# K of a group in one load of 64 KB rows: three neighbouring pages, and a branch on TensorE that picks the second

## The chip, the cores and the metric

The kernel runs on one core of a Trainium2 chip, as one launch. The metric is the device time of that launch in microseconds (us).

## The reference

One decode step (one token, D = 512) of a gated mix of two blocks: attention over a long cache, and a SwiGLU feed-forward block.

```python
g = sigmoid((x * gate_w).sum(-1, keepdims=True))
q = (x @ wq)                      # 32 heads of 128; 8 groups, 4 heads share one K and V
scores = einsum(q, k) * 128**-0.5 # k_cache: 8 groups x 32768 positions x 128, bf16
o = einsum(softmax(scores), v)    # v_cache: the same shape
a = o @ wo                        # wo: 4096 x 512
b = (silu(x @ w_gate) * (x @ w_up)) @ w_down
out = g * a + (1 - g) * b         # 1 x 1 x 512, bf16
```

K and V of one group are 8 MB each (32768 x 128 in bf16), so 128 MB of the 148 MB that the kernel reads are the two caches.

## The kernel before, in words

**Tiling.** A group's K is seen as 128 partitions of 256 positions each, in two halves b = 0, 1 of R = 128 positions per partition. One half of one tensor is a *page*: 32 KB in each partition, 4 MB. The tile `page` holds five pages. K has pages 0 and 1 (`PG_K`), one for each half; V has pages 2 and 3 (`PG_V`); w_gate and w_up start in page 3 (`PG_F`), and page 4 (`PG_X`) holds wq first and wo at the end.

**Loads.** All come from SyncE's queue (SP), in an order written by hand: wq, x, gate_w, w_gate, w_up; then for each group g K half 0, K half 1 (`load_k(g, b)`, L263), V (`load_v(g)`, L274, one load of both pages; the last group's V is two loads, L280); then w_down (L295) and wo in five parts (L301). SP waits before a load until its page is free: `load_k(g, b)` waits for the fill that ends half b of group g-1 (`sem_fill`), and `load_v(g)` waits until TensorE has ended the V matmuls of group g-1 (`sem_v_free`). A wait on SP holds every load behind it.

**A group on the engines.** TensorE (`emit_k`, once for each half) takes a half in UPP = 8 units. A unit is a *fill* (`emit_fill`, L309: 8 transposes of 128 x 128 FP32 words, each a pair of bf16 values, into one of two PSUM tiles `pst`) and, LAG = 2 units later, its *scores* (`emit_scores`, L321: 16 small matmuls into the PSUM bank `ps_sc[b]`). Between them VectorE copies the PSUM tile into `ktT` (L635). Each half ends with two units of scores alone, since its last two copies have to come back first. VectorE then takes the half's maximum (L640). After both halves come the maximum over partitions (`emit_max`: L343, L347 on TensorE with L650, L654 on VectorE between), the bias `nbias` on ScalarE (L516), eight exponentials of 128 x 128 on ScalarE (L523, four for each half), 64 V matmuls of 128 x 512 (`emit_v`, L362), and a small reduction (`emit_reduce`: L374, L383). TensorE works strictly in this order, so a group's fills begin after the reduction of the group before.

**Loops.** TensorE, VectorE and ScalarE each run the eight groups as a loop in registers, `Fori(0, G*STEP, STEP)` with STEP = 16; semaphores count on, and a wait compares with the loop's register plus a constant. TensorE's code for the end (`emit_end`: w_down, L214, and the first part of wo) stands ahead of that for the start in the program, and is reached in a second turn of an outer loop.

**The end.** w_down's matmuls, the scaled heads (L668, L678, L685, L687), the matmuls with wo in five parts (L214, L225), one ScalarE copy (L697), one VectorE copy (L699) and the output's load to DRAM (L701).

Of the kernel before, what the change touches and what calls it, by code (L numbers as in the profile page):

```python
# [5 lines left out]
ACT = mybir.ActivationFunctionType  # L6
ALU = mybir.AluOpType
# [5 lines left out]
def bass_gated_mix__gqa_block_cached__swiglu_ffn__decode_kernel(  # L13
# [26 lines left out]
    R = 128  # L40
# [27 lines left out]

    PG_K = (0, 1)
    PG_V = 2  # L70
    PG_F = 3
    PG_X = 4
    NPG = 5

    with ExitStack() as es:
# [57 lines left out]
        def T(name, shape, dt):  # L133
            return es.enter_context(nc.sbuf_tensor(name, shape, dt))
# [26 lines left out]
        nbias = T("nbias", [128, HPG], FP32)  # L161
        esum = T("esum", [128, NB, HPG], FP32)
        esum2 = T("esum2", [128, HPG], FP32)
        acc = T("acc", [128, RQ, DH], FP32)
# [10 lines left out]

        ps_sc = [P(f"ps_sc{i}", [128, 512], FP32) for i in range(NB)]
        ps_o = P("ps_o", [128, 512], FP32)
# [27 lines left out]

        vpage = page[:, PG_V : PG_V + NB, :].rearrange("p b (r d) -> p b r d", d=DH)
        wq_v = page[:, PG_X, 0 : KC * H * DH].rearrange("p (c n) -> p c n", c=KC)
        wgu = page[:, PG_F, 0 : 2 * KC * F].rearrange("p (w c f) -> p w c f", w=2, c=KC)
# [39 lines left out]
        with nc.Block("main") as block:  # L248
            @block.gpsimd
            def _(pool):  # L250
                pool.memset(ones_f[:, :], 1.0).then_inc(sem_ones, 1)
                pool.memset(ones_bf[:, :], 1.0).then_inc(sem_ones, 1)
                for g in range(G - 1):
                    pool.wait_ge(sem_v[0], 16 * (g + 1))
                    pool.sem_inc(sem_v[1], 16)

            @block.sync
            def _(sp):
                def load_k(g, b):
                    if g:  # L260
                        sp.wait_ge(sem_fill, UPG * (g - 1) + UPP * (b + 1))
                    src = A_k_cache[0, g, :, :].rearrange("(p b r) d -> p b r d", b=NB, r=R)
                    sp.dma_start(  # L263
                        page[:, PG_K[b], :].rearrange("p (r d) -> p r d", d=DH), src[:, b, :, :]
                    ).then_inc(sem_k[b], 16)

# [24 lines left out]
                for g in range(G):  # L291
                    for b in range(NB):
                        load_k(g, b)
                    load_v(g)
                sp.dma_start(  # L295
                    wd[:, :, :], B_w_down.rearrange("(p j) n -> p j n", j=FC)
# [7 lines left out]
            def _(pe):  # L304
                def emit_fill(b, u):
                    kv = page[:, PG_K[b], :].bitcast(FP32)
                    for k in range(RPU):
                        n = u * RPU + k
                        ins = pe.transpose(  # L309
                            pst[u % NST][:, k * 128 : (k + 1) * 128],  # L310
                            kv[:, n * 128 : (n + 1) * 128],
                            ident_f[:, :],
                        )
                    ins.then_inc(sem_fill, 1)
# [14 lines left out]

                def emit_k(i, b):  # L330
                    pe.wait_ge(sem_k[b], i + 16)
                    for u in range(UPP + LAG):
                        if u >= LAG:
                            pe.wait_ge(sem_cp, i + (UPP * b + u - LAG + 1))
                        if u < UPP:
                            emit_fill(b, u)
                        if u >= LAG:
                            ins = emit_scores(b, u - LAG)
                    ins.then_inc(sem_sc, UPP)

# [51 lines left out]
                def emit_start():  # L392
# [86 lines left out]
                    with pe.Fori(0, G * STEP, STEP) as i:  # L479
                        for b in range(NB):  # L480
                            emit_k(i, b)
                        emit_max(i)
                        emit_v(i)
                        emit_reduce(i)
# [21 lines left out]
            def _(act):  # L506
# [5 lines left out]
                act.activation(sg, pst[1][:, 0:FS], ACT.Sigmoid).then_inc(sem_act_sg, 1)  # L512

                with act.Fori(0, G * STEP, STEP) as i:
                    act.wait_ge(sem_b, i + STEP)
                    act.activation(  # L516
                        nbias[:, :], ps_m[:, M_B0 : M_B0 + HPG], ACT.Copy, scale=-SCALE
                    ).then_inc(sem_nbias, STEP)
                    act.wait_ge(sem_nbias, i + STEP)
                    for b in range(NB):  # L520
                        sc = ps_sc[b][:, :].rearrange("p (t h) -> p h t", h=HPG)
                        for h in range(HPG):
                            act.activation(  # L523
                                ET[:, b * R : (b + 1) * R, h],
                                sc[:, h, :],
                                ACT.Exp,
# [8 lines left out]
            def _(dve):  # L535
# [95 lines left out]
                with dve.Fori(0, G * STEP, STEP) as i:  # L631
                    for b in range(NB):
# [101 lines left out]
```

## Time and profile before

| what | value |
|---|---|
| median of 3 runs | 351.63 us (351.47 to 351.8) |
| the profiled execution's own time | 351.67 us |
| its span in the profile | 350.4 us (the other 1.27 us lie around it) |
| DMA queue of SP | 148.12 MB, 98.4% of 16 engines' span; 423 GB/s mean |
| TensorE matmul / weight load busy | 73% / 60% |
| VectorE, ScalarE busy | 55%, 12% |
| mean granted TensorE clock | 0.864 of full speed |

The table's shares are means over the whole span. What ends last differs from stage to stage, and within a group TensorE's, VectorE's and ScalarE's work is a chain: a share of 73% does not say how long that chain is.

### The profile page before, as it was taken

How to read it: one execution, taken by the hardware profiler on the slowest of the kernel's cores; microseconds unless marked ns; L12 is line 12 of the kernel's file. 1: busy time of each engine (PE TensorE's matmuls, PEld its weight loads, DVE VectorE, ACT ScalarE, POOL GpSimd, SP SyncE). 2: the span in 40 equal slices, each digit the busy share in tenths (PEclk: the TensorE clock that was granted, in tenths of full speed). 3: DMA queues.
4: the chain of work that ended last, by engine and by line, in shares of the span. 5: the costliest groups of instructions: out<-in, count | busy, mean ns of one | idle time of the engine just before them, and what ended most of it. 6: DMA issues, size and time to landing. Idle time of an engine off the chain costs nothing.

```text
span 350.4 us, 8660 instructions
## 1 busy us (share of the span) xinstructions
PE 254.6 (73%) x3871; PEld 209.2 (60%) x3871; DVE 192.1 (55%) x242; ACT 42.9 (12%) x156; POOL 0.4 (0%) x6
## 2 busy tenths in 40 slices
PE   1443986688857994898858993798768893798574
PEld 1113985288725984398726991498627891498431
DVE  4243986068803885068804892088705891198500
ACT  1000000400050002300050005000050005000130
POOL 0000000000000000000000000000000000000000
PEclk9965999699968997689969997889859995899878
DMA  8999999999989999999999999999999999999995
GB/s 337 408 451 419 477 443 384 423 430 456 464 385 417 456 426 430 423 464 434 434 404 419 464 449 400 423 449 434 434 419 419 464 434 415 423 426 434 420 423 205
DMA packets 4914, 148.21 MB, mean 423 GB/s; under 512 B 554, under 2 KB 556, under 8 KB 940
## 3 DMA queue, kind: packets, MB, share of 16 engines
q1 hardware_dynamic: 4908, 148.12, 98.4%
q8 instruction: 5, 0.08, 0.1%
q14 instruction: 1, 0.01, 0.0%
HBM read 148.11 MB, written 0.00 MB: 423 GB/s over the span
## 4 chain that ended last, share of the span: by engine, by line
DMA 69%; PE 25%; DVE 3%; SPq 1%; ACT 1%; issue 1%; DVEq 0%; ACTq 0%
DMA page<-in_A_k_cache_dram 56%; PE pst L309 18%; DMA page<-in_A_wo_dram 12%; PE ps_sc L321 5%; DVE ktT L635 2%; PE ps_o L362 2%; SPq L301 0%; ACT ET L523 0%; ACT L516 0%; SPq L288 0%; SPq L280 0%; DVE pmaxf L640 0%; PE ps_m L347 0%; SPq L295 0%; PE ps_sc L225 0%
## 5 line engine op out<-in xcount | busy, mean ns | idle before, releaser
L635 DVE COPY ktT<-pst 128x2048 bf16<-128x2048 bf16 x128 | 155.4, 1223 | 31.1 <-PE pst L309 23.4
L309 PE MATMUL pst<-ident_f,page 128*128 128x128 f32 x1024 | 140.5, 286 | 15.6 <-DMA page<-in_A_k_cache_dram 10.3
L309 PEld LDWEIGHTS pst<-ident_f,page 128*128 128x128 f32 x1024 | 115.9, 146 | 19.8 <-DMA page<-in_A_k_cache_dram 11.0
L321 PE MATMUL ps_sc<-qcur,ktT 128*128 128x8 bf16 x2048 | 67.8, 166 | 8.6 <-DVE ktT L635 8.6
L321 PEld LDWEIGHTS ps_sc<-qcur,ktT 128*128 128x128 bf16 x2048 | 66.7, 97 | 11.2 <-DVE ktT L635 10.0
L362 PE MATMUL ps_o<-page,ET 128*16 128x512 bf16 x512 | 43.6, 515 | 27.1 <-ACT ET L523 27.1
L362 PEld LDWEIGHTS ps_o<-page,ET 128*16 128x16 bf16 x512 | 15.8, 113 | 51.5 <-issue 36.4
L516 ACT ACT_TABLE_LOAD x8 | 10.3, 1283 | 239.0 <-PE ps_m L347 239.0
L658 DVE TENSOR_TENSOR esum<-esum 128x4 f32<-128x4 f32 x8 | 1.3, 164 | 42.7 <-ACT ET L523 42.7
L523 ACT ACTIVATE ET<-ps_sc,nbias 128x128 bf16<-128x128 f32 x64 | 23.9, 562 | 0.7
L662 DVE RECIPROCAL rS<-ps_sc 128x4 f32<-128x4 f32 x8 | 1.5, 182 | 34.2 <-PE ps_sc L374 34.2
L523 ACT ACTIVATION_READ_ACCUMULATOR ET<-ps_sc,nbias 128x1 f32 x64 | 18.6, 290 | 0.0
L640 DVE TENSOR_REDUCE pmaxf<-ps_sc 128x4 f32<-128x512 f32 x16 | 11.1, 692 | 10.4 <-PE ps_sc L321 10.4
L383 PE MATMUL ps_m<-sel,acc 128*128 128x4 f32 x64 | 8.4, 255 | 3.6 <-ACT acc L532 3.6
L383 PEld LDWEIGHTS ps_m<-sel,acc 128*128 128x128 f32 x64 | 7.7, 191 | 4.3 <-ACT acc L532 4.3
L343 PE MATMUL ps_m<-ident_f,pmax 128*4 128x128 f32 x8 | 2.5, 308 | 9.1 <-DVE pmax L642 9.1
L532 ACT ACTIVATE acc<-ps_o 128x512 f32<-128x512 f32 x8 | 4.8, 597 | 34.5 <-PE ps_o L362 34.5
L347 PE MATMUL ps_m<-diag,ones_f 4*128 4x4 f32 x16 | 3.6, 294 | 6.3 <-DVE diag L654 6.3
L347 PEld LDWEIGHTS ps_m<-diag,ones_f 4*128 4x128 f32 x16 | 3.2, 244 | 8.1 <-issue 8.1
L404 PE MATMUL ps_m<-ones_bf,x_row 1*128 1x1 bf16 x4 | 0.3, 172 | 9.3 <-DMA x_row<-in_A_x_dram 9.3
L343 PEld LDWEIGHTS ps_m<-ident_f,pmax 128*4 128x4 f32 x8 | 0.6, 81 | 9.6 <-issue 9.6
L404 PEld LDWEIGHTS ps_m<-ones_bf,x_row 1*128 1x128 bf16 x4 | 0.2, 114 | 9.6 <-DMA x_row<-in_A_x_dram 9.6
(68 smaller groups left out, 53.8 us busy)
## 6 DMA issues: line engine op xcount, KB each, us to landing
page<-in_A_k_cache_dram SPq DMA_DIRECT2D x16, 4096.0 KB, 27.4
page<-in_A_v_cache_dram SPq DMA_DIRECT2D x2, 4096.0 KB, 27.3
page<-in_A_wq_dram SPq DMA_DIRECT2D x1, 4096.0 KB, 12.3
page<-in_A_wo_dram SPq DMA_DIRECT2D x1, 2048.0 KB, 40.2
page<-in_B_w_gate_dram SPq DMA_DIRECT2D x1, 1792.0 KB, 15.5
page<-in_B_w_up_dram SPq DMA_DIRECT2D x1, 1792.0 KB, 19.4
wd<-in_B_w_down_dram SPq DMA_DIRECT2D x1, 1792.0 KB, 35.8
page<-in_A_wo_dram SPq DMA_DIRECT2D x1, 1024.0 KB, 42.3
```

The lines of the kernel that those rows point to most:

```text
L309: ins = pe.transpose(pst[u % NST][:, k * 128 : (k + 1) * 128], kv[:, n * 128 : (n + 1) * 128], ident_f[:, :],)
L321: ins = pe.matmul(ps_sc[b][:, col : col + 2 * HPG], kt[:, k, e, :], qcur[:, e, :], start=(e == 0), stop=(e == 1),)
L343: pe.transpose(ps_m[0:HPG, M_A0 : M_A0 + 128], pmax[:, :], ident_f[:, :]).then_inc(sem_t, STEP)
L347: pe.matmul(ps_m[:, M_B0 : M_B0 + HPG], ones_f[0:HPG, :], diag[:, :], start=True, stop=True,).then_inc(sem_b, STEP)
L362: ins = pe.matmul(ps_o[32 * c : 32 * c + RQ * HPG, :], ET[:, n : n + RQ, :].rearrange("p n h -> p (n h)"), vpage[:, b, k * RQ : (k + 1) * ...
L383: ins = pe.matmul(ps_m[:, M_P0 : M_P0 + HPG], acc[:, q, :], sel4[:, q * HPG : (q + 1) * HPG], start=(q == 0), stop=(q == RQ - 1),)
L516: act.activation(nbias[:, :], ps_m[:, M_B0 : M_B0 + HPG], ACT.Copy, scale=-SCALE).then_inc(sem_nbias, STEP)
L523: act.activation(ET[:, b * R : (b + 1) * R, h], sc[:, h, :], ACT.Exp, bias=nbias[:, h : h + 1], scale=SCALE, accum_out=esum[:, b, h : h + ...
L532: act.activation(part, ps_o[:, :], ACT.Copy).then_inc(sem_acc, STEP)
L635: dve.tensor_copy(ktT[:, u % NKT, :], pst[u % NST][:, :].bitcast(BF16)).then_inc(sem_cp, 1)
L640: dve.tensor_reduce(pmaxf[:, b, :], sc, AX.X, ALU.max).then_inc(sem_d, 1)
L662: dve.reciprocal(rS[:, :], ps_s).then_inc(sem_d, 1)
```

## The change

K of a group becomes one load of both halves, with 64 KB rows, for the groups 0 to 6. K now moves among three neighbouring pages A, B, C (0, 1, 2): an even group lies in B and C, an odd group in A and B. Page B is always worked on first. So in an odd group half 1 (page B) comes first and half 0 (page A) second. V and the feed-forward weights move up by a page, wq lies in page A and wo in page C.

- `load_k(g)` waits for the fill that ends the first-worked half of group g-1 (the same value as half 0's wait before). The last group's K is still two loads, half 1 first; the second waits for one more fill.
- GpSimd raises `sem_k[1]` when the whole load has raised `sem_k[0]`, as it did for V.
- SP waits for the fills of the groups 0 to 6 before w_down, because wo now lies in a page of K.
- TensorE runs one pipeline over 18 steps for both halves: the LAG of the first half is no longer drained at the half's end, so that unit 6's and 7's scores come after the fills 8 and 9. The second half's code stands twice in the loop, one copy for page C and one for page A, each behind an `If` on the loop register's parity.
- ScalarE picks the PSUM bank of each exponential by a register (`odd`), since the bank of half 0 changes with parity.
- `nbias` moves from ScalarE (`ACT.Copy`) to VectorE, behind `diag`; a dummy exponential (`eone`) ahead of ScalarE's loop. In the built program the activation-table load that stood in ScalarE's loop, ahead of `nbias`, now stands once ahead of the loop. Each of the eight exponentials gets a register instruction ahead of it.

```diff
-    PG_K = (0, 1)
-    PG_V = 2
-    PG_F = 3
-    PG_X = 4
+    PG_A, PG_B, PG_C = 0, 1, 2
+    PG_V = 3
+    PG_F = 4
+    PG_Q = PG_A
+    PG_X = PG_C
...
-        ps_sc = [P(f"ps_sc{i}", [128, 512], FP32) for i in range(NB)]
+        ps_all = P("ps_sc", [128, NB, 512], FP32)
+        ps_sc = [ps_all[:, b, :] for b in range(NB)]
...
                 for g in range(G - 1):
-                    pool.wait_ge(sem_v[0], 16 * (g + 1))
-                    pool.sem_inc(sem_v[1], 16)
+                    for s in (sem_k, sem_v):
+                        pool.wait_ge(s[0], 16 * (g + 1))
+                        pool.sem_inc(s[1], 16)
...
-                def load_k(g, b):
+                def load_k(g):
                     if g:
-                        sp.wait_ge(sem_fill, UPG * (g - 1) + UPP * (b + 1))
+                        sp.wait_ge(sem_fill, UPG * (g - 1) + UPP)
+                    lo = PG_A if g % 2 else PG_B
+                    dst = page[:, lo : lo + NB, :].rearrange("p b (r d) -> p b r d", d=DH)
                     src = A_k_cache[0, g, :, :].rearrange("(p b r) d -> p b r d", b=NB, r=R)
-                    sp.dma_start(
-                        page[:, PG_K[b], :].rearrange("p (r d) -> p r d", d=DH), src[:, b, :, :]
-                    ).then_inc(sem_k[b], 16)
+                    if g < G - 1:
+                        sp.dma_start(
+                            dst.rearrange("p b r d -> p (b r d)"),
+                            src.rearrange("p b r d -> p (b r d)"),
+                        ).then_inc(sem_k[0], 16)
+                    else:
+                        for n, b in enumerate((1, 0)):
+                            if n:
+                                sp.wait_ge(sem_fill, UPG * (g - 1) + UPP + 1)
+                            sp.dma_start(dst[:, b, :, :], src[:, b, :, :]).then_inc(
+                                sem_k[n], 16
+                            )
...
                 for g in range(G):
-                    for b in range(NB):
-                        load_k(g, b)
+                    load_k(g)
                     load_v(g)
+                sp.wait_ge(sem_fill, UPG * (G - 1))
...
-                def emit_k(i, b):
+                def emit_k(i, b, pg):
                     pe.wait_ge(sem_k[b], i + 16)
-                    for u in range(UPP + LAG):
-                        if u >= LAG:
-                            pe.wait_ge(sem_cp, i + (UPP * b + u - LAG + 1))
-                        if u < UPP:
-                            emit_fill(b, u)
-                        if u >= LAG:
-                            ins = emit_scores(b, u - LAG)
-                    ins.then_inc(sem_sc, UPP)
+                    for n in range(UPP * b, UPP * (b + 1) + LAG * (b == NB - 1)):
+                        if n >= LAG:
+                            pe.wait_ge(sem_cp, i + (n - LAG + 1))
+                        if n < UPG:
+                            emit_fill(pg, n % UPP)
+                        if n >= LAG:
+                            ins = emit_scores((n - LAG) // UPP, (n - LAG) % UPP)
+                            if (n - LAG) % UPP == UPP - 1:
+                                ins.then_inc(sem_sc, UPP)
...
-                        for b in range(NB):
-                            emit_k(i, b)
+                        emit_k(i, 0, PG_B)
+                        with pe.If((i & STEP) < 1):
+                            emit_k(i, 1, PG_C)
+                        with pe.If((i & STEP) > 0):
+                            emit_k(i, 1, PG_A)
...
+                act.wait_ge(sem_ones, 2)
+                act.activation(eone[:, :], ones_f[:, 0:1], ACT.Exp)
...
-                    act.wait_ge(sem_b, i + STEP)
-                    act.activation(
-                        nbias[:, :], ps_m[:, M_B0 : M_B0 + HPG], ACT.Copy, scale=-SCALE
-                    ).then_inc(sem_nbias, STEP)
                     act.wait_ge(sem_nbias, i + STEP)
+                    odd = (i & STEP) * (R // STEP)
+                    sc = ps_all[:, :, :].rearrange("p b (t h) -> p h (b t)", h=HPG)
                     for b in range(NB):
-                        sc = ps_sc[b][:, :].rearrange("p (t h) -> p h t", h=HPG)
+                        bank = R - odd if b else odd
...
-                                sc[:, h, :],
+                                sc[:, h, bass.ds(bank, R)],
...
+                    dve.wait_ge(sem_b, i + STEP)
+                    dve.tensor_scalar(
+                        nbias[:, :], ps_m[:, M_B0 : M_B0 + HPG], -SCALE, None, op0=ALU.mult
+                    ).then_inc(sem_nbias, STEP)
```

More of the change, by code (lines that the diff above doesn't have):

```diff
@@ L67, in bass_gated_mix__gqa_block_cached__swiglu_ffn__decode_kernel @@
     assert QT == 2 and QN == 512 and F % (NSTRIP * FC) == 0 and FS <= 512
-    PG_K = (0, 1)
-    PG_V = 2
-    PG_F = 3
-    PG_X = 4
+    PG_A, PG_B, PG_C = 0, 1, 2
[3 more added lines that the diff above has]
+    PG_X = PG_C
     NPG = 5
+    assert G % 2 == 0
     with ExitStack() as es:
@@ L162, in bass_gated_mix__gqa_block_cached__swiglu_ffn__decode_kernel @@
         esum = T("esum", [128, NB, HPG], FP32)
+        eone = T("eone", [128, 1], FP32)
         esum2 = T("esum2", [128, HPG], FP32)
@@ L206, in bass_gated_mix__gqa_block_cached__swiglu_ffn__decode_kernel @@
         vpage = page[:, PG_V : PG_V + NB, :].rearrange("p b (r d) -> p b r d", d=DH)
-        wq_v = page[:, PG_X, 0 : KC * H * DH].rearrange("p (c n) -> p c n", c=KC)
+        wq_v = page[:, PG_Q, 0 : KC * H * DH].rearrange("p (c n) -> p c n", c=KC)
         wgu = page[:, PG_F, 0 : 2 * KC * F].rearrange("p (w c f) -> p w c f", w=2, c=KC)
@@ L304, in _, with emit_fill @@
             def _(pe):
-                def emit_fill(b, u):
-                    kv = page[:, PG_K[b], :].bitcast(FP32)
+                def emit_fill(pg, u):
+                    kv = page[:, pg, :].bitcast(FP32)
                     for k in range(RPU):
```

## The prediction

> **What bounds the kernel now.** The page first: the DMA queue is busy 98.4% of the span at 423 GB/s, so up to some late point the loads set the time.
>
> ```profile
> span 350.4 us, 8660 instructions
> ...
> q1 hardware_dynamic: 4908, 148.12, 98.4%
> ```
>
> Then the timeline of SP's issues beside the DMA issues with time to landing, asked for short windows. Group 6's K halves, issued at 237.91 and 249.69, landed 27.7 and 25.6 us later, at 265.6 and 275.3; V, issued at 263.53, landed 31.2 us later, at 294.7; group 7's first half (275.75 + 28.7) at 304.4. A half takes 9.7 us, V's 8 MB take 19.4, a group 38.8.
>
> ```profile
> 249.69 0.33 SPq L263 DMA_DIRECT2D page<-in_A_k_cache_dram  x1
> ...
> 263.53 0.33 SPq L274 DMA_DIRECT2D page<-in_A_v_cache_dram  x1
> ```
>
> Third, stretches (us, PE, PEld, DVE, ACT, POOL busy, clock, DMA share, GB/s), each from a group's first fill to the end of its reduction: how long TensorE's chain through a group really is.
>
> ```profile
> 110.44:149.07 38.63, 31.32 (x461) 25.97 (x461) 22.24 (x25) 5.04 (x19) 0.00 (x0) 0.82 1.00 432
> ...
> 265.65:302.99 37.34, 29.61 (x461) 24.75 (x461) 22.15 (x25) 5.04 (x19) 0.00 (x0) 0.86 1.00 434
> 304.46:341.13 36.67, 28.94 (x465) 24.66 (x469) 22.15 (x25) 5.04 (x19) 0.00 (x0) 0.91 1.00 428
> ```
>
> The eight of them have a mean of 37.6 us (36.67 to 38.63, the longer at the lower clock) against 38.8 of loading. TensorE is busy for 30 of these, but has hardly more than 1 us to spare: it starts on a group when the first half lands and is done just before the next group's lands. This chain is the second bound, and it matters where it starts.
>
> Last, the timeline at a seam between two halves, and at the end.
>
> ```profile
> 122.80 0.56 PE L321 MATMUL ps_sc<-qcur,ktT 128*128 128x8 bf16 x16 [0.54 <-DVE ktT L635]
> ...
> 123.39 0.69 DVE L640 TENSOR_REDUCE pmaxf<-ps_sc 128x4 f32<-128x512 f32 x1 [0.65 <-PE ps_sc L321]
> 124.32 3.63 DVE L635 COPY ktT<-pst 128x2048 bf16<-128x2048 bf16 x3 [0.24 <-PE pst L309]
> ```
>
> ```profile
> 342.93 1.03 PE L214 MATMUL ps_sc<-page,O 128*1 128x512 bf16 x16 [0.71 <-DMA page<-in_A_wo_dram]
> ...
> 347.93 0.38 PE L225 MATMUL ps_sc<-page,O 128*1 128x128 bf16 x8 [0.29 <-DMA page<-in_A_wo_dram]
> 348.36 0.29 DVE L699 CAST res_row<-ps_sc 128x128 bf16<-128x128 f32 x1 [5.91 <-PE ps_sc L225]
> ```
>
> Group 7 is done at 341.1, and its matmuls with wo then wait for DMA (0.71, 1.38, 0.67 and 0.29 us idle): the end is the loads' too, but TensorE has only about 3 us in hand.
>
> **The change, part by part.**
>
> *64 KB rows.* K's two halves of 32 KB rows took 19.4 us, V's load with 64 KB rows 19.4. To one decimal there is nothing to gain; rounding leaves 0 to 0.1 us for each of seven loads. I take 0.05, 0.3 us by group 6.
>
> *One landing in place of two.* The fills wait for the whole load. Before, group 6's began at 265.65, with half 0. Now they begin when half 1's bytes are in: 275.3 less 0.3, so 275.0, 9.4 us later. In the groups 0 to 5 this costs nothing while the chain fits within a period, since each start moves by the same.
>
> *SP's order.* `load_k(g+1)` now waits for one value, eight fills into group g, 10.1 to 11.3 us after its start (275.75 - 265.65; 121.51 - 110.44). V of group g then has 8 us to run: the queue is fed. `load_v(g+1)` waits for the V matmuls of group g, 35.0 to 36.9 us after its first fill (223.01 - 188.04; 147.30 - 110.44). Before, 13 us of loads were still queued at that point; now the next K ends 38.8 us after the fills began, so 1.9 to 3.9 us are queued. Behind this wait on SP stand all later loads. The output's load of 1 KB was issued at 348.68 and SP waited 1.0 us for it, so a load needs at most 1.6 us from issue to landing: the queue just doesn't run dry. I take no cost, with 1 us for the upper end; the cover is thin (a rival below).
>
> *Mid-group seam.* The row at 122.80 was TensorE's wait for the last copy (0.54), after which the reduce (0.69) and the next copy ran. This drain goes. But VectorE still reduces half 0 before it copies unit 8, and unit 7's scores now stand behind fill 9. Copy 7 ends at 122.74 as before; fill 9 follows in the steady rhythm of 1.31 us a unit (fill 7 at 120.40, so fill 9 at 123.0), and its scores end 1.46 us later, at 124.5 instead of 123.36. Reduce 0.69 and a step of 0.1: copy 8 starts at 125.3 instead of 124.32. TensorE has filled both `pst` tiles and waits for that copy. The seam gets 1.0 us longer. Bounds: 1.6 us shorter (all of the gap between copy 7 and copy 8 gone), 1.5 longer; I take 1.0, since it follows from rows in this very stage.
>
> *The two `If`s.* The page shows no branch. Its nearest row is the loop's own: group 2's reduction ended at 149.07 and fills began at 149.25, so a branch back with its register work costs at most 0.2 us. The first `If` adds 0 to 0.3 us ahead of fill 8; those at the end lie beside TensorE's wait for the second maximum (1.14 us in front of L343). I take 0.1 a group; if the code has to be fetched, see below.
>
> *`nbias` and the table load.* The group of the table loads on the page, and one of them in the timeline:
>
> ```profile
> L516 ACT ACT_TABLE_LOAD x8 | 10.3, 1283 | 239.0 <-PE ps_m L347 239.0
> ```
>
> ```profile
> 138.07 1.28 ACT L516 ACT_TABLE_LOAD   x1 [30.63 <-PE ps_m L347]
> ...
> 139.63 0.54 ACT L523 ACTIVATE ET<-ps_sc,nbias 128x128 bf16<-128x128 f32 x1
> ```
>
> From L347's end (137.99) to the first exponential it is 1.64 us, of which the table load is 1.28. On VectorE the same step costs about what L668 costs (0.16) and two handovers of 0.05 to 0.1, and the register work of ScalarE's first bank some 0.1: 0.4 in all. The chain gets 1.2 us shorter. The other register instructions lie beside exponentials that follow each other every 0.35 us. The single table load and dummy exponential now ahead of the loop lie in ScalarE's idle time before group 0.
>
> *The rest* (GpSimd's wait and raise, 16 more in all on an idle engine; SP's wait ahead of w_down, already met because V of group 7 waited for more): nothing.
>
> **The sum.** A group's chain: 37.6 + 1.0 + 0.1 - 1.2 = 37.5 us, inside the loads' 38.8 by 1.3. So the groups 0 to 6 keep the loads' pace. Group 6 starts at 275.0 and ends at 312.5. Group 7's first half has landed by then (304), its second at 314, well ahead of its use: nothing is left to wait for, and it runs from 312.6 to 350.1, where before it ended at 341.13. By that time w_down and wo are in (they landed up to 347.6, and are issued behind a V load that the queue takes without a gap). So the end runs without its waits: the strips and the head chain to 342.5 on the old clock, then 1.03, a gap of 0.5 at the end of the block (0 to 1.38, the row that names the load), 0.60, 0.60 on ScalarE, 0.39, 0.35, 0.38 with steps of 0.05: VectorE's last copy at 346.6 instead of 348.36, and 2.0 from there to the span's end as before. That is 7.4 us behind the end of the reduction. 350.1 + 7.4 = 357.5 us of span. The profiled execution took 351.67, 1.27 more than its span, and stands 0.04 over the median: 357.5 + 1.27 = 358.8, say **358.7**.
>
> [...]
>
> The low end: both groups at 36.67 - 0.2, the start at 274.4, no gap at the end of the block: 355.3. The high end: both at 38.7, a start 1 us late: 362.5.
>
> **The rivals.**
>
> *The code no longer stays at hand.* The loop grows from 461 to 685 pairs of weight load and matmul, and each pass jumps over one copy of 224 pairs. For: a jump over that much is new here. Against: eight passes needed few fetches in all.
>
> ```profile
> q8 instruction: 5, 0.08, 0.1%
> ```
>
> If each jump has to fetch 16 KB (0.08 MB over 5), an engine at 26 GB/s takes 0.6 us, behind at most a 64 KB row of 2.5: 0.6 to 3.1 a jump. With some 2.5 a pass beyond what the wait hides, a group takes 40.0, more than its loads. TensorE sets the pace from its first fill, at 42.6 when the whole first K is in: 42.6 + 8 x 40.0 + 7.4 + 1.3 = 371. It decides from 38.8 a group.
>
> [...]
>
> *V is issued too late.* If the V matmuls end 1 us or more later than I have it, the 1.9 to 3.9 us of queue go, and the queue pauses once a group, by about half of what the chain is over. At 1 us for six groups: 358.7 + 6 = 365.
>
> *Faster.* The seam could shrink instead of growing: with the pipeline closed, 1.5 us go, the table load's 1.2 too, and at group 7's clock a group takes 36.7 - 2.7 = 34.0. Then 275.0 + 68.0 + 7.4 + 1.3 = 351.7, no change; with 0.1 more from each 64 KB row, 351.0, a little faster. It decides when groups 6 and 7 together take under 67.5 us. Against: VectorE's reduce stands between copies 7 and 8 in both orders.
>
> *The rows bring nothing.* That is in the forecast.
>
> **How the numbers follow.** The forecast's mechanism 0.80; fetches at each pass 0.07; a dry queue 0.07; the shortened chain 0.06, half of it on either side of no change. A measurement can tell about 0.2% from no change. Range 355.3 to 362.5: it leaves out the fetches, most of the dry queue and the gain. Slower 0.94, same 0.03, faster 0.03.
>
> **What would show it.** Right: the fills of groups 0 to 6 start when a whole K has landed (near 42.6 and then every 38.8), group 7's follow group 6's reduction with no DMA wait, at 312 to 313; DVE's idle time ahead of the first-half reduce rises from 0.65 to about 1.7; no table load in the groups; no DMA wait in front of the matmuls with w_down and wo, and a DMA share near zero in the last 8 us. Wrong: a first fill of group 7 before 309, TensorE's chain over 38.8, gaps in the DMA share between groups, or more than about ten instruction packets.

## The result, and the profile after

The changed kernel takes 371.23 us (median of 6, 368.54 to 374.75) against 351.64 before, a ratio of 1.0537 (95% interval 1.0497 to 1.0578). The forecast was 358.7, its range 355.3 to 362.5: right in direction, and 12.5 us short. The profile below is of the slowest of the six (374.75 us), which the ratio leaves out as over 1.5% above the fastest, as the medians further down leave out one execution of a_no_miss (385.62) and one of a_halves (435.8). A second profiled execution (374.27, among the experiments) has the same stages: its groups start within 1.5 us of the ones below.

The page's lines on the span, the load queue and the code fetches:

```profile
span 373.4 us, 8750 instructions
...
q1 hardware_dynamic: 3900, 148.12, 92.9%
q8 instruction: 7, 0.11, 0.1%
```

The queue is no longer busy throughout, and seven packets of code were fetched where there had been five. Next, the groups as before, from first fill to the end of the reduction (us, PE, PEld, DVE, ACT, POOL busy, clock, DMA share, GB/s):

```profile
42.47:90.09 47.62, 33.30 (x462) 28.70 (x463) 22.22 (x26) 3.61 (x17) 0.00 (x0) 0.76 0.83 351
89.95:126.88 36.93, 29.52 (x463) 24.56 (x462) 22.38 (x27) 3.61 (x17) 0.00 (x0) 0.91 0.99 428
...
287.88:327.89 40.01, 32.99 (x462) 27.75 (x463) 22.22 (x26) 3.61 (x17) 0.00 (x0) 0.79 0.95 405
327.75:366.75 39.00, 31.59 (x467) 27.14 (x470) 22.38 (x27) 3.61 (x17) 0.00 (x0) 0.82 0.84 358
```

Group 0 starts at 42.5, as forecast, but takes 47.6 us. The groups 1 to 7 have a mean of 38.7 (36.93 to 40.01), about as long as a group's loads. Group 6 starts at 287.9 instead of the 275.0 of the forecast; group 7 follows it without a pause, as forecast.

What happened in group 0, in its timeline (start, duration, engine and instruction, idle time before it and what ended it) and in two stretches of it:

```profile
79.26 0.37 PE L360 MATMUL ps_m<-ident_f,pmax 128*4 128x128 f32 x1 [7.67 <-issue]
...
88.32 0.33 SPq L290 DMA_DIRECT2D page<-in_A_v_cache_dram  x1
```

```profile
73.00:82.00 9.00, 0.92 (x3) 0.57 (x3) 0.66 (x3) 0.56 (x3) 0.00 (x0) 0.50 0.63 266
82.00:92.00 10.00, 8.35 (x90) 4.72 (x90) 1.67 (x5) 3.05 (x15) 0.00 (x0) 0.79 0.31 105
```

TensorE stood for 7.67 us ahead of the maximum, "issue": nothing that the page counts held it. The trace's record of the sequencer has a branch of 8.0 us there: the jump from the end of the even copy over the odd one, with two code packets inside it and a third right behind. The V load of group 1 waited for this group's V matmuls and left at 88.32. K of group 1 had landed at 81.4 (issued at 53.49, 27.9 to landing), and behind it the queue was empty: the share of 0.31.

The end is TensorE's, as forecast:

```profile
366.75:373.40 6.65, 3.56 (x79) 1.45 (x79) 1.05 (x5) 0.60 (x1) 0.00 (x0) 0.97 0.01 3
```

### The profile page after: what moved, and what is told of

Read it like the earlier page. It is cut to its first block, busy times and chain, and to the rows that moved or that the text cites. A ratio compares the mean times of both kernels' runs of the same rounds, so it can differ in the third digit from the quotient of the medians.

```text
span 373.4 us, 8750 instructions
## 1 busy us (share of the span) xinstructions
PE 267.4 (72%) x3871; PEld 222.2 (59%) x3871; DVE 192.7 (52%) x250; ACT 33.0 (9%) x142; POOL 0.4 (0%) x6
## 5 line engine op out<-in xcount | busy, mean ns | idle before, releaser
L656 DVE COPY ktT<-pst 128x2048 bf16<-128x2048 bf16 x128 | 155.4, 1223 | 49.2 <-PE pst L325 42.6
L325 PE MATMUL pst<-ident_f,page 128*128 128x128 f32 x1024 | 154.2, 302 | 35.4 <-DMA page<-in_A_k_cache_dram 18.7
L325 PEld LDWEIGHTS pst<-ident_f,page 128*128 128x128 f32 x1024 | 126.7, 156 | 37.8 <-DMA page<-in_A_k_cache_dram 19.2
L337 PEld LDWEIGHTS ps_sc<-qcur,ktT 128*128 128x128 bf16 x2048 | 70.0, 98 | 7.9 <-DVE ktT L656 5.0
L337 PE MATMUL ps_sc<-qcur,ktT 128*128 128x8 bf16 x2048 | 69.6, 167 | 5.1 <-DVE ktT L656 4.3
L379 PE MATMUL ps_o<-page,ET 128*16 128x512 bf16 x512 | 44.4, 522 | 17.0 <-ACT ET L544 17.0
L544 ACT ACTIVATE ET<-ps_sc,nbias 128x128 bf16 x64 | 24.1, 561 | 275.3 <-DVE nbias L679 275.3
L661 DVE TENSOR_REDUCE pmaxf<-ps_sc 128x4 f32<-128x512 f32 x16 | 11.1, 692 | 20.6 <-PE ps_sc L337 20.6
L671 DVE TENSOR_REDUCE gm<-ps_m 4x1 f32<-4x128 f32 x8 | 2.2, 279 | 9.8 <-PE ps_m L360 9.8
```

Source lines behind the costliest of these rows:

```text
L325: ins = pe.transpose(pst[u % NST][:, k * 128 : (k + 1) * 128], kv[:, n * 128 : (n + 1) * 128], ident_f[:, :],)
L337: ins = pe.matmul(ps_sc[b][:, col : col + 2 * HPG], kt[:, k, e, :], qcur[:, e, :], start=(e == 0), stop=(e == 1),)
L379: ins = pe.matmul(ps_o[32 * c : 32 * c + RQ * HPG, :], ET[:, n : n + RQ, :].rearrange("p n h -> p (n h)"), vpage[:, b, k * RQ : (k + 1) * ...
L544: act.activation(ET[:, b * R : (b + 1) * R, h], sc[:, h, bass.ds(bank, R)], ACT.Exp, bias=nbias[:, h : h + 1], scale=SCALE, accum_out=esum ...
L656: dve.tensor_copy(ktT[:, u % NKT, :], pst[u % NST][:, :].bitcast(BF16)).then_inc(sem_cp, 1)
L661: dve.tensor_reduce(pmaxf[:, b, :], sc, AX.X, ALU.max).then_inc(sem_d, 1)
```

## The experiments

My theory after this result had three parts: the late start on a group, which the end pays; one fetch in group 0; and a longer chain, because the longer seam between the halves idles TensorE and the clock falls behind it. The rivals were a dry queue that alone sets the time, and branches that cost in every pass.

A group has 16 copies from PSUM, counted from 0 as the units are: copy 7 is the first half's last, copy 8 the second half's first. "Copy 16's end" means the end of the sixteenth, the last.

**The fetch, made to happen early (a_no_miss).**

```diff
+                def emit_groups():
...
-                with pe.Fori(0, 2, 1) as turn:
-                    with pe.If(turn > 0):
+                with pe.Fori(0, 3, 1) as turn:
+                    with pe.If(turn > 1):
                         emit_end()
                     with pe.If(turn < 1):
                         emit_start()
+                    with pe.If((turn & 1) > 0):
+                        emit_groups()
```

> The changed kernel with one edit: TensorE's outer loop has three turns (start, groups, end), so that TensorE jumps once over the whole group loop, to the code behind the second copy, while it waits for the first K. Theory 1 (the first jump over the second copy fetches its target and takes 8 us in group 0, once; the V load of group 1 is then issued 8 us late and the queue runs empty): group 0's chain falls from 47.6 us to about 39.5, the V load of group 1 is issued near 80 instead of 88.3, the hole in the DMA share at 75 to 92 us goes, and the time falls by 7 to 8 us, to about 363 (361 to 366). Rival A (the fetch is hidden; a dry queue in every group, from a chain over 38.8 us, makes the time): group 0 shortens, but the time falls by under 3 us, since the later groups set the pace anyway. Rival B (each pass fetches code): the branch behind the even copy still takes several us in later groups, and the time stays near 371.

Measured: 372.39 us (368.32 to 372.9). The edit did not do what it was for. The trace has the early jump (8.6 us at 29.2, while TensorE had nothing to do), ten code packets instead of seven, and still a branch of 6.7 us in group 0, whose chain was 45.5 us. So the early jump did not spare TensorE this one, and the run says nothing on the fetch's price, but no later pass has a branch of more than 0.3 us: rival B is out.

**VectorE takes the first maximum later (a_reduce_late).** The two copies that TensorE waits for go first.

```diff
-                    for b in range(NB):
-                        for u in range(UPP):
...
-                        dve.wait_ge(sem_sc, i + UPP * (b + 1))
-                        sc = ps_sc[b][:, :].rearrange("p (t h) -> p h t", h=HPG)
-                        dve.tensor_reduce(pmaxf[:, b, :], sc, AX.X, ALU.max).then_inc(sem_d, 1)
...
+                    for n in range(UPG):
...
+                        if n in (UPP + 1, UPG - 1):
+                            b = n // UPG if n < UPG - 1 else 1
+                            dve.wait_ge(sem_sc, i + UPP * (b + 1))
+                            sc = ps_sc[b][:, :].rearrange("p (t h) -> p h t", h=HPG)
+                            dve.tensor_reduce(pmaxf[:, b, :], sc, AX.X, ALU.max).then_inc(sem_d, 1)
```

> The changed kernel with one edit: VectorE copies units 8 and 9 before it takes the first half's maximum. Theory 1 (the seam idles TensorE for over 2 us, and behind that idle time the granted clock halves for 3.4 us or more in the second half's fills): the gap between copy 7 and copy 8 falls from 2.4 us to under 0.5, with about 0.6 lost once behind copy 9; the stretch from copy 8's start to copy 16's end, 10.2 to 12.9 us now, is about 11 (one reduce more in it) in every group and no longer varies; the chain of a group falls from a mean of 38.7 (groups 1 to 7) to 36.5 to 37; time about 364 (362 to 367), group 0's 8 us still in it. Rival (the second half is slow because its code stands elsewhere or behind a branch, or the clock falls anyway): the seam gets shorter by 1.5 us, but the slow stretches in the second half stay, the chain is over 37.5, and the time 367 to 369.

Measured: 357.17 us (355.42 to 358.7), 14 us below the changed kernel by this alone, and below the 362 to 367 that I had expected. VectorE at the seam of group 1 in the changed kernel, and of group 2 here:

```profile
103.06 0.69 DVE L661 TENSOR_REDUCE pmaxf<-ps_sc 128x4 f32<-128x512 f32 x1 [1.80 <-PE ps_sc L337]
103.67 2.34 DVE L656 COPY ktT<-pst 128x2048 bf16<-128x2048 bf16 x2
```

```profile
133.98 7.79 DVE L656 COPY ktT<-pst 128x2048 bf16<-128x2048 bf16 x6
141.68 0.68 DVE L663 TENSOR_REDUCE pmaxf<-ps_sc 128x4 f32<-128x512 f32 x1
142.28 4.94 DVE L656 COPY ktT<-pst 128x2048 bf16<-128x2048 bf16 x4
```

The wait of 1.80 us is gone: copies, reduce and copies follow each other. From copy 8's start to copy 16's end it is 10.6 us in each of the groups 1 to 7, 0.4 more than the undisturbed 10.2, since a reduce lies in it, and their mean chain is 35.7. Of the 3.0 us by which it is shorter, the gap between copy 7 and copy 8 makes 2.3 (2.4 to 0.1) and the second half 0.8 (11.4 to 10.6). That gives TensorE 3 us a group in hand again, and the loads set the pace from group 1 on (group 6 starts at 281.1, five groups after group 1's 86.4). Of the 16.0 us between the two profiled spans, 3.6 come before group 1's start, 3.2 in the groups 1 to 5 and 9.2 in the groups 6 and 7.

**K in halves for every group (a_halves).** Pages, branches, seam and registers stay. GpSimd no longer raises `sem_k[1]`, since each half now has its own load.

```diff
...
-                    if g < G - 1:
-                        sp.dma_start(
-                            dst.rearrange("p b r d -> p (b r d)"),
-                            src.rearrange("p b r d -> p (b r d)"),
-                        ).then_inc(sem_k[0], 16)
-                    else:
-                        for n, b in enumerate((1, 0)):
+                    for n, b in enumerate((1, 0) if g % 2 else (0, 1)):
+                        if n and g:
...
```

> The changed kernel with one edit: K of every group comes in two loads of 4 MB with 32 KB rows, the half that is worked on first ahead, each with a semaphore of its own, as the last group's does in the changed kernel. Theory 1 (one landing in place of two delays TensorE's start on a group by 9.7 us, and the end pays it): group 0's fills start near 32.8 instead of 42.5; group 0 still takes its 8 us for the fetch; then TensorE goes from group to group without waiting for K, at 38 to 38.7 us each, and ends group 7 near 349 to 351; time 356 to 360. Rival (the time is set by a dry queue and late V loads, whatever the landings are): time over 365, with gaps in the DMA share in every group.

Measured: 351.61 us, as before (ratio 1.0008, 0.9997 to 1.0019). With two landings nothing of the 19.6 us is left.

```profile
32.71:78.68 45.97, 33.37 (x462) 28.56 (x463) 22.31 (x26) 3.61 (x17) 0.00 (x0) 0.76 1.01 431
115.57:154.49 38.92, 31.51 (x464) 27.10 (x464) 22.38 (x27) 3.61 (x17) 0.00 (x0) 0.82 1.00 433
...
304.62:344.00 39.38, 31.98 (x467) 26.41 (x470) 22.38 (x27) 3.61 (x17) 0.00 (x0) 0.83 0.99 424
344.00:350.67 6.67, 3.56 (x79) 1.45 (x79) 1.05 (x5) 0.60 (x1) 0.00 (x0) 1.00 0.39 149
```

Group 0 still has its slow branch (7.1 us, chain 46.0) and the chains of the groups 1 to 7 are 38.0 on average, but TensorE starts at 32.7, goes from there through all eight groups without a wait for K, and the queue stays busy (1.01, 1.00, 0.99): the V load of group 1 left at 76.9, with K still in the queue. I had expected 356 to 360. TensorE ended group 7 at 344.0 and not at 349 to 351: group 0 was done 2 us earlier, and TensorE, which never waited for K, took 11.3 us to the end of copy 7 in each of the groups 1 to 7, the shortest in any of these profiles. That the time is the kernel before's to 0.03 us is in part luck: in the profiled execution (352.08) TensorE, and no longer the loads, ends last (344.0 + 6.67), so it has nothing in hand.

**The same, but TensorE waits for both halves (a_halves_wait).** One wait added to a_halves:

```diff
                 def emit_k(i, b, pg):
+                    if b == 0:
+                        pe.wait_ge(sem_k[1], i + 16)
                     pe.wait_ge(sem_k[b], i + 16)
```

> The kernel with K in two loads for every group (a_halves), with one edit: TensorE waits for both halves before its first fill of a group. The loads, their rows of 32 KB and their order stay. Theory 1 (the late start on a group is the whole cost; it also makes TensorE wait for each K and so lowers its clock): back to the time of the changed kernel, 371 (366 to 375), fills of group 0 from 42.5, chains of 38 to 39.5. Rival (the 64 KB rows of K harm, through what they hold up in the DMA engines): under 356.

Measured: 373.34 us (372.85 to 374.26). This single wait brings back all of it, with rows of 32 KB. The rival, that the long rows harm, is out. Three of its groups:

```profile
42.39:88.10 45.71, 32.77 (x462) 28.40 (x463) 22.32 (x26) 3.59 (x17) 0.00 (x0) 0.76 0.88 369
127.85:167.02 39.17, 32.22 (x462) 28.20 (x463) 22.32 (x26) 3.59 (x17) 0.00 (x0) 0.81 1.01 427
...
325.71:364.97 39.26, 32.30 (x465) 28.22 (x469) 22.32 (x26) 3.59 (x17) 0.00 (x0) 0.81 0.81 345
```

Group 0 starts at 42.4, and the share of 0.88 is the hole behind its late V load. Group 2 starts 2.9 us after group 1's end, and its clock is 0.81.

**Only the seam (b_seam)**, in the kernel before:

```diff
-                    for u in range(UPP + LAG):
+                    for n in range(UPP * b, UPP * (b + 1) + LAG * (b == NB - 1)):
...
+                            ins = emit_scores((n - LAG) // UPP, (n - LAG) % UPP)
```

> The kernel before with one edit: TensorE's pipeline of 18 steps over both halves (unit 6's and 7's scores behind the fills 8 and 9), without pages that move, branches, or any other part of the change. Theory 1 (the seam itself lengthens the chain by 0.8 us, and the clock falls behind it): gap between copy 7 and copy 8 2.4 us instead of 1.6; the second half's copies take 11.5 us in most groups instead of 10.2; the chain is 38.5 to 39.5 us instead of 37.6 and TensorE sets the pace: 354 to 359. Rival (no effect of the seam on the clock): chain 38.4, still within the loads' 38.8, time 351.6 to 352.5.

Measured: 351.56 us: the rival's time, but not all of its mechanism, since the clock did fall in some groups (0.85 from 202.4 to 213.6 us, a second half). VectorE at a seam:

```profile
84.29 1.22 DVE L636 COPY ktT<-pst 128x2048 bf16<-128x2048 bf16 x1
87.30 0.69 DVE L641 TENSOR_REDUCE pmaxf<-ps_sc 128x4 f32<-128x512 f32 x1 [1.78 <-PE ps_sc L321]
87.90 1.21 DVE L636 COPY ktT<-pst 128x2048 bf16<-128x2048 bf16 x1
```

The gap between copy 7 and copy 8 is 2.39 us instead of 1.58, as expected, but the second half slowed down in only two of the groups 1 to 7 (11.5 us against 10.2) and in group 0. The chain of the groups 1 to 7, 38.3 on average, still fits the loads' 38.8.

**Only the bias and the table load (b_bias)**, in the kernel before:

```diff
...
+                act.wait_ge(sem_ones, 2)
+                act.activation(eone[:, :], ones_f[:, 0:1], ACT.Exp)
...
                 with act.Fori(0, G * STEP, STEP) as i:
-                    act.wait_ge(sem_b, i + STEP)
-                    act.activation(
-                        nbias[:, :], ps_m[:, M_B0 : M_B0 + HPG], ACT.Copy, scale=-SCALE
-                    ).then_inc(sem_nbias, STEP)
...
+                    dve.wait_ge(sem_b, i + STEP)
+                    dve.tensor_scalar(
+                        nbias[:, :], ps_m[:, M_B0 : M_B0 + HPG], -SCALE, None, op0=ALU.mult
+                    ).then_inc(sem_nbias, STEP)
```

> The kernel before with one part of the change alone: nbias on VectorE and the table load ahead of ScalarE's loop. Theory 1 (the loads set the time before, and TensorE's chain is not on the path as long as it is under 38.8): the chain falls by 1.2 us to about 36.4, copy 16's end to the first exponential from 4.8 to 3.6, and the time stays, 351.3 to 351.8. Rival (part of the chain lies bare in the end): 350.5 or less.

Measured: 351.65 us. Copy 16's end to the first exponential fell from 4.8-5.1 to 3.5-3.8 us, as forecast, in time that nobody waited for. The chain did not follow: its mean over the eight groups is 37.3 and not the expected 36.4. The first halves took 0.45 us longer on average and the stretch behind the first exponential 0.5. TensorE's waits between the groups had grown from 7.4 to 10.2 us in all, which may be why: the point on the clock below shows what a wait does to a first half.

**No long jumps (a_small_if).** The second half's fills stand twice, unit by unit, and the scores once:

```diff
+                def emit_k2(i):
+                    pe.wait_ge(sem_k[1], i + 16)
+                    for n in range(UPP, UPG + LAG):
+                        if n < UPG:
+                            with pe.If((i & STEP) < 1):
+                                pe.wait_ge(sem_cp, i + (n - LAG + 1))
+                                emit_fill(PG_C, n % UPP)
+                            with pe.If((i & STEP) > 0):
+                                pe.wait_ge(sem_cp, i + (n - LAG + 1))
+                                emit_fill(PG_A, n % UPP)
+                        else:
+                            pe.wait_ge(sem_cp, i + (n - LAG + 1))
+                        ins = emit_scores((n - LAG) // UPP, (n - LAG) % UPP)
+                        if (n - LAG) % UPP == UPP - 1:
+                            ins.then_inc(sem_sc, UPP)
...
-                        with pe.If((i & STEP) < 1):
-                            emit_k(i, 1, PG_C)
-                        with pe.If((i & STEP) > 0):
-                            emit_k(i, 1, PG_A)
+                        emit_k2(i)
```

> The changed kernel with one edit: each of the second half's eight fills stands twice behind its own pair of branches, and the scores once, so that no jump is longer than 8 pairs of weight load and matmul; the waits stand behind the branches. Theory 1 (group 0's one fetch costs 7 to 8 us there, and delays the V load of group 1 and all that follows): no branch of several us, group 0's chain 39 to 40 instead of 47.6, V of group 1 issued at 79 to 81 instead of 88, later chains as in the changed kernel (38 to 39.5), time 364 (361 to 367). Rival (the dry queue and the chains set the time, the fetch is absorbed): 369 to 372.

Measured: 368.4 us (364.53 to 369.46). Group 0's chain is 42.2 instead of 47.6, with branches of at most 1.7 us and five code packets, and V of group 1 leaves at 82.7. I had expected 39 to 40 for that chain and 361 to 367 for the time. Since the executions spread, the changed kernel and this one were run once more on one chip:

> The changed kernel itself once more, on one chip beside a_small_if, since their medians so far (371.2 and 368.4) come from different chips and runs that spread over 4 to 6 us. Theory 1 (the one fetch in group 0 is worth 3 to 6 us at the end): 369 to 373, and 3 us or more above a_small_if. Rival (it is absorbed, and the difference was the clock's spread): within 1.5 us of a_small_if.

> The kernel with short jumps once more, beside the changed kernel. Theory 1: 366 to 368.5, 3 us or more below it. Rival: within 1.5 us of it.

Measured: 372.59 us (369.72 to 374.27) and 368.32 (367.14 to 370.31). The fetch is worth 4.3 us between these medians, though the ranges overlap by 0.6, and group 0's chain lost about as much in the two profiles (47.1 to 42.4). From copy 16's end to the first exponential group 0 still takes 6.1 us there, against 10.6 in the changed kernel and 3.6 to 4.0 in later groups.

**Short jumps and the late maximum together (a_small_late):** the edits of a_small_if and a_reduce_late.

> a_small_if with VectorE's late reduce of a_reduce_late as well: neither the fetch nor the long seam. Theory 1: chains of 35.5 to 36.2, groups 0 to 6 at the loads' pace, group 6 from 275, group 7 from 311, its reduction ends near 345.5, and the end of the program follows 6.7 us behind: 352.5 to 354. Against a_reduce_late's 357.2 the difference is the fetch in group 0, 3.5 to 5 us. Rival (16 branches a group cost TensorE): chains over 37, time over 356.

Measured: 357.37 us (355.51 to 359.33), no better than a_reduce_late's 357.17, though the profiled execution (355.51; chain of group 0 39.2, group 6 from 276.2, 1.2 us later than expected) was. I had expected 352.5 to 354. Why the other executions took 1.4 to 3.8 us more than the profiled one no record here shows, and so what the fetch is worth in this form stays open.

**A version that could beat both (a_mix):** a_small_late, with K in halves for the groups 5 to 7 only.

```diff
-                    for s in (sem_k, sem_v):
+                    for s in (sem_k, sem_v) if g < G - 3 else (sem_v,):
...
-                    if g < G - 1:
+                    if g < G - 3:
...
-                        for n, b in enumerate((1, 0)):
+                        for n, b in enumerate((1, 0) if g % 2 else (0, 1)):
```

> A version that could beat both: a_small_late (short jumps, late reduce) with K of the groups 0 to 4 in one load of 64 KB rows and of the groups 5 to 7 in halves, the first-worked half ahead. Theory 1: the chain of 35.7 us leaves 3 us a group, so TensorE is back on the loads' heels once halves land; group 7 starts near 304 and the end is the loads' again; the 64 KB rows of five groups save at most 0.1 us each: 351.0 to 351.7. Rival (TensorE does not catch up in three groups, or the queue pauses for late V loads in the groups 1 to 4): 352.5 to 355.

Measured: 356.15 us (353.46 to 357.51). I had expected 351.0 to 351.7. In the profiled execution (353.46) TensorE caught up as expected (chains of 34.5 in groups 5 and 6, without a wait), but group 7's K landed at 306.2 and not at 304.4: the loads themselves had lost 1.8 us by then, and the one stretch with a low DMA share is that of group 1:

```profile
82.13:121.92 39.79, 29.19 (x463) 24.69 (x463) 22.44 (x28) 3.60 (x17) 0.00 (x0) 0.89 0.97 422
121.92:160.63 38.71, 31.15 (x461) 26.95 (x462) 22.37 (x27) 3.60 (x17) 0.00 (x0) 0.85 1.00 433
```

Its V load left at 80.49, 0.6 us before the K load ahead of it had landed (81.06), and landed 21.4 us behind that K instead of the usual 19.4.

With five whole landings left it is 4.5 us slower than the kernel before, whatever their rows save. No version here beats that kernel.

**A jump alone (b_jump)**, in the kernel before:

```diff
                         for b in range(NB):
                             emit_k(i, b)
+                        with pe.If((i & STEP) > STEP):
+                            emit_k(i, 1)
                         emit_max(i)
```

> The kernel before with one edit: a copy of the second half's code (192 pairs of weight load and matmul) stands between the halves and the maximum, behind a branch that is never taken, so that each pass jumps over it. Theory 1 (the first such jump fetches its target, once, and is absorbed where 13 us of loads are queued): group 0's chain rises by 6 to 8 us to 44 to 46, one slow branch and no other, the groups after it start late and catch up, time 351.4 to 352.5. Rival (a late group 0 is not made up): 355 or more.

Measured: 351.62 us, but the expected stall did not come: group 0's chain is 39.1 and no branch was slow: TensorE's idle time ahead of the eight maxima is 9.1 us in all, as in the kernel before. A jump over 192 pairs cost nothing that shows here, the first one over 224 pairs in the changed kernel took 8.0 us; whether the length decides or the place of the target, no run here shows. So this run shows nothing on what the queue's cover absorbs; a_halves does, whose group 0 took 7.1 us for its branch at no cost in the end.

## Why the prediction was wrong, point by point

**Where the 16 us of the span went.** The forecast's span was 357.5, the profiled one 373.4. Group 1 started at 89.95, and by the forecast's pace it would have been 42.6 + 38.8 = 81.4: 8.6 us. From there to group 6 it is 197.9 for five groups, 39.6 each instead of 38.7: 4.3. Groups 6 and 7 took 78.9 instead of 75.1: 3.8. The end took 6.65 instead of 7.4: -0.8. In sum 15.9. Two of the signs of being wrong appeared: chains over 38.8 (in five of the eight groups) and a gap in the DMA share.

**The step that failed** is the first sentence under the sum: "a group's chain: 37.6 + 1.0 + 0.1 - 1.2 = 37.5 us, inside the loads' 38.8 by 1.3. So the groups 0 to 6 keep the loads' pace." The chain measured 38.7 in the groups 1 to 7 and 47.6 in group 0. Before, the groups 1 to 7 had 37.5: the seam added 0.8, the second half 1.2 and the first half 0.2, and the bias took 1.1 off. The terms, one by one:
- *The seam, +1.0.* Nearly right, it is 0.8: 1.8 us of wait in front of the first maximum (1.7 forecast), the gap between the copies 2.4 instead of 1.6.
- *`nbias` and the table load, -1.2.* Right: copy 16's end to the first exponential took 4.8 to 5.1 us before and 3.6 to 4.0 after, group 0 aside.
- *The clock (the sum takes the mean chain of before, 37.6).* Mis-sized, and the largest part in the groups 1 to 7. At the seam TensorE used to stand idle in two short pieces (0.54 us in the prediction's row at 122.80, and the first row here); now it does so in one piece (the second row, of group 6 in the changed kernel):

```profile
125.60 1.09 PE L309 MATMUL pst<-ident_f,page 128*128 128x128 f32 x8 [0.45 <-DVE ktT L635]
```

```profile
303.96 1.29 PE L325 MATMUL pst<-ident_f,page 128*128 128x128 f32 x8 [1.92 <-DVE ktT L656]
```

  Two stretches from copy 8's start to copy 16's end in the changed kernel, groups 1 and 2:

```profile
103.67:113.85 10.18, 8.44 (x160) 8.28 (x160) 9.68 (x9) 0.00 (x0) 0.00 (x0) 1.00 0.95 412
144.84:156.51 11.67, 9.92 (x160) 9.68 (x160) 9.69 (x9) 0.00 (x0) 0.00 (x0) 0.85 1.04 449
```

  With a clock of 0.85 the same work takes 1.5 us longer. With the gap of 1.6 us (before, b_bias, b_jump) this stretch was 10.2 us in all 24 groups; with the gap of 2.4 it was longer in 5 of the groups 1 to 7 of the changed kernel, 6 of 7 in a_halves, 2 of 7 in b_seam, and in 38 of 56 over all eight profiles with this gap; with no gap (the three kernels with the late maximum) it was 10.6 in all 21. That the longer gap lets the clock fall is shown; that it does so in some groups and not in others is not explained by it. The mean rose from 10.2 to 11.4. A wait for K does the same to the first half:

```profile
89.95:101.26 11.31, 10.87 (x174) 10.55 (x174) 9.86 (x9) 0.00 (x0) 0.00 (x0) 1.00 0.87 377
129.66:142.45 12.79, 12.79 (x173) 12.70 (x174) 9.80 (x8) 0.00 (x0) 0.00 (x0) 0.83 0.95 410
```

  Group 1 followed group 0 without a pause; group 2 came after 2.8 us of waiting for its K. Behind 1.92 us of idle time in one piece the granted clock was 0.50 for 3.41 us in group 2 (147.71 to 151.12) and in group 6 (304.72 to 308.13), and the stretches took 11.7 and 11.5 us. The same idle time in group 1, ahead of 104.93, was followed by 1.00 (the first of the two stretches above). The sum had no lower clock for the idle time that its own seam term added. Its low end has 36.67 for both group 6 and group 7, the chain of group 7 in the kernel before; no run shows the two at that figure, and in the profile above they took 40.0 and 39.0.
- *The `If`s, 0.1 a group.* The later passes show no branch of more than 0.3 us, but the term was wrong by 6.6 us in the first: with a branch of 8.0 us, copy 16's end to the first exponential took 10.5 there, against 3.6 to 4.0. My rival had the mechanism, but a price of 0.6 to 3.1 us a jump, from the length of one packet behind another, and a fetch in each pass. It was one stall, of 8 us, with two packets in it. That the rival's time was 371 is a coincidence: it had the chain at 40.0 in every group for a reason that the seven packets and the other branches refute.

**A late V load, "I take no cost".** Wrong from the first group on: the cover of 1.9 to 3.9 us was thin, group 0's branch overran it, and the queue stood empty. And the cover that a V load needs was mis-read from the output's load of 1 KB, 1.6 us. In the fourteen profiles, from group 1 on, a V load that left 2.95 us or more ahead of the landing of the K before it landed 19.3 to 19.7 us behind that K; of the 21 that left 0.6 to 2.6 us ahead, 19 landed 19.8 to 22.2 us behind it. (This is from each trace's issue and landing times.) In the profile above V of the groups 2 to 6 left 4.5, 1.2, 3.6, 2.6 and 2.6 us ahead, and the second, fourth and fifth of them landed 20.2 to 20.9 us behind. Why a shorter lead costs this much stays open. My rival of a V that is issued too late had this mechanism, at a chance of 0.07. The two things I took apart, a chain inside the period and a queue that is fed, are one: with a whole K to land, a chain that comes near to the loads' period delays V, V delays the next K, and TensorE waits for that K at a clock that falls (2.8 us of waiting in front of group 2, whose first half ran at 0.83).

**"9.4 us later" for the start, paid at the end.** The mechanism is right and larger than forecast. Between a_halves and a_halves_wait, one wait apart, the spans differ by 21.0 us: 9.7 in group 0's start, 8.7 in waits between groups, which a_halves has none of, and 2.6 in longer chains. The ends are alike. So this wait accounts for the whole 19.6 us: the longer seam and the stall in group 0 cost nothing at the median of a_halves, and cost time only where TensorE starts on a whole K.

**The 64 KB rows.** About right. In the kernel before, the two halves of group 6's K landed 19.44 us behind the load ahead of them, its V 19.36 behind K; a whole K in the changed kernel (group 3) landed 19.35 behind V. That is 0.08 us a load, 0.05 forecast; a_mix shows that it doesn't pay for five late landings.

**Slower, 0.94.** Right. The range was too narrow above: it held the chain at 38.7 and a start 1 us late, when group 6's start was 12.9 late. Its two ends add up to 355.5 and 362.2 from the terms that are named, and 121.51 - 110.44 is 11.1 and not 11.3 (group 3 has 11.3); neither matters to the miss.

## What to carry to other kernels

In this kernel a merged load gained nothing, because the consumer could start on its first half: merging moved the consumer's start by half a load, and took the same half out of the lead with which the next loads are issued (V of group 1 left at 76.9 in a_halves, at 86.3 in a_halves_wait). Before adding work to an engine whose chain is 97% of the period, ask what sets its clock, and what a single late pass does to a queue with 2 to 4 us in it. Time taken out of a chain that then waits may not stay out: b_bias took 1.2 us out of one step, and the chain shrank by 0.3. Where an engine waits for a copy, let the helper do the copy before its other work: one reduce in the wrong place was worth 14 us here, where K landed whole, and nothing in b_seam, where it landed in halves.

## What the runs showed of the hardware that was not expected

The first jump over 224 pairs of weight load and matmul took 7.1 to 8.2 us while the loads ran (a DMA share of 0.94 from 71.1 to 79.1 us in the changed kernel; 8.0 and 8.2 us in the changed kernel, 7.7 in a_reduce_late, 7.1 and 7.2 in the kernels with halves), and the later ones 0.3 us at most; over 192 pairs, in b_jump, no jump was slow, and TensorE's idle time ahead of the eight maxima was 9.1 us, as before the change. A jump made ahead of time over the whole loop did not spare it (6.7 us).

A gap of 2.4 us between copies 7 and 8, with 1.92 us of idle time on TensorE in the changed kernel, was followed by a longer second half in 38 of 56 groups (in group 6 of the changed kernel with 3.41 us at a granted clock of 0.50); behind two pieces of 0.54 and 0.45 us it was 10.2 us in all 24.

A V load that left 0.6 to 2.6 us before the load ahead of it had landed came 0.4 to 2.9 us late in 19 of 21 cases; one that left 2.95 us or more before came at most 0.4 late.
